# Half-row token products, a new order of the products, block 0's values turned on TensorE, and three MLP products moved forward, in a recurrent-memory transformer kernel

## The chip, the cores and the metric

One core of one Trainium2 chip. The time is the device time of one execution in microseconds (us). Medians of 3 to 6 timed executions are given, and one profiled execution of each kernel shows where the time lies (the one execution that was traced, so a stage of it can be unlucky). A ratio is the mean time of one kernel's fast runs over that of the other's in the same rounds, so it isn't quite the ratio of the medians quoted beside it.

## The reference, cut to what matters

```python
def _A_ref(x, mem0, Wq, Wk, Wv, Wo, seg_len):      # seg_len 32, 64 segments
    mem = mem0                                      # 8 memory rows
    for s in range(n_seg):
        h = concatenate([mem, x[:, s*32:(s+1)*32]])  # 40 rows of 512
        q, k, v = h @ Wq, h @ Wk, h @ Wv            # 32 heads of 128
        p = softmax(where(mask, q @ k.T * scale, -1e9))
        o = (p @ v) @ Wo
        mem = o[:, :8]                              # carried to the next segment
        outs.append(o[:, 8:])
h  = x + _A_ref(layernorm(x), ...)
h2 = h + gelu(layernorm(h) @ w1 + b1) @ w2 + b2     # MLP with 1792 inner columns
```

The segments form a chain through `mem`. The 64 segments come in 16 blocks of four (one block is 128 tokens). I call the four segments of a block its first to fourth.

## The kernel before

The kernel records every operation with its reads and writes, and a list scheduler places them on the five engines. TensorE's own order is fixed by hand in `ORDER`: Q0, K0, Q1, K1 are the projections (two halves of the heads), SC0 and SC1 the scores with the memory rows, SA the self scores of the tokens, V0 and V1 the value projections, PV0 and PV1 the value products of the memory rows, PVA the value product of the tokens (of the segment before), WO the output projection, and F a filler: projections for the next block, or WO of the last rows.

```python
PHASE = (109, 215, 114, 200)     # place of a segment's start within 256 instructions
ORDER = (("Q0", 0, 4), ("K0", 0, 4), ("Q1", 0, 4), ("K1", 0, 4), ("SC0", 0, 99), ("V0", 0, 4), ("V1", 0, 2), ("SC1", 0, 99), ("SA", 0, 99), ("V1", 2, 4), ("F",
         0, 2), ("PV0", 0, 99), ("F", 2, 3), ("PV1", 0, 99), ("WO", 0, 8), ("PVA", 0, 99), ("F", 3, 4))
# [...]
        def pv_a(s):                         # token value product: 8 pairs on the full array
            par = s % 3
            def f(e):
                for k in range(8):
                    ins = e.matmul(rows_a(k), VS[:, par, k // 4, (k % 4) * E:(k % 4 + 1) * E], BD[:, s % 2, k // 2, :, :, k % 2],
                                   start=(s == NS - 1 and k % 2 == 0), stop=True, skip_group_check=True)
                return ins
            S.op("pe", f, reads=[...], writes=QK, dur=0.45, mode=MF, ni=16)
# [...]
        def pv_a_ev(s):                      # one eviction of 768 columns
            ...
            S.either(copy2(ot, src, 768), reads=QK, writes=[("OTx", opar)])
# [...]
    def align(self):    # counts TensorE's instructions; pads the first passes of a segment with
        ...             # repeated weight loads until the count is PHASE[segment % 4] modulo 256
# [...]
        S.op("pool", lambda e: e.memset(maskR[:], 0.0), writes=["maskR"])   # then 18 affine selects
# [...]
            S.op("pool", lambda e: e.tensor_scalar(rs, ag[:, 1:2], 1e-5, None, ALU.add), ...)  # layer norm
```

`BONUS` adds a tuned number to the scheduler's priority for each kind of tile.

## Time and profile before

| | before |
|---|---|
| median of the runs | 850.03 us (849.67 to 851.71, 3 runs; 850.87 with a fourth) |
| span of the profiled run | 851.0 us, mean granted clock 0.990 |
| segment 4 starts at | 89.36 us |
| period of segments 4 to 59, mean / shortest | 10.88 / 10.68 us |
| segment 63 and the MLP tail | 118.67 us |

The prediction shows the lines behind this. They are read as start, duration, engine, source line, output<-input, partitions x columns, count. The bracket at the end is the engine's idle time before the row and what ended it; "issue" there means that the engine waited for nothing that the profile knows. Because matmuls overlap (in the trace of before a WO group starts at 303.31 and lasts 1.93 us, to 305.24, and the token product after it starts at 305.18), the distance between two starts (the advance) counts, not the duration.

### The profile page before, as it was taken

To read this page: it belongs to the slowest core of one execution; us is meant where nothing else is said; L and a number is where in the kernel's file an instruction comes from. 1 tells how busy PE (TensorE), PEld (TensorE's weight loads), DVE (VectorE), ACT (ScalarE), POOL (GpSimd) and SP (SyncE) were. 2 spreads that over 40 slices of the span, in tenths; PEclk is the share of its full clock that TensorE was granted. 3 is DMA by queue.
4 is the path that set the end of the run, shared out by engine and by line. 5 is a ranking of instruction groups with operands and counts; after the bars stand their busy time and mean duration, and the time that the engine had idled before them with its cause. 6 is when DMAs were issued, how large, how long until landed. Compare 5 with 4: busy or idle time off the path is not lost.

```text
span 851.0 us, 47411 instructions
## 1 busy us (share of the span) xinstructions
PE 801.9 (94%) x20061; PEld 438.9 (52%) x22307; DVE 566.5 (67%) x1818; ACT 553.2 (65%) x1561; POOL 265.3 (31%) x686
## 2 busy tenths in 40 slices
PE   3668999999999999999999999999999998999998
PEld 1245555555555555555555555555555555544443
DVE  3257677878787878777778777777777776633111
ACT  2446777767776767777777777777777776742442
POOL 5023114242424242424242333323232313166200
PEclk9979999999999999999999999999999999999999
DMA  9961000110101010101010101010112121274100
GB/s 344 361 193 22 10 17 22 30 29 23 35 20 38 17 40 16 35 22 35 23 35 22 35 23 35 17 29 17 28 35 54 47 72 35 70 195 111 50 25 25
DMA packets 66615, 48.80 MB, mean 57 GB/s; under 512 B 29156, under 2 KB 62828, under 8 KB 66412
## 3 DMA queue, kind: packets, MB, share of 16 engines
q1 hardware_dynamic: 66080, 45.50, 18.4%
q8 instruction: 166, 2.72, 1.3%
q10 hardware_dynamic: 332, 0.27, 0.1%
q14 instruction: 37, 0.30, 0.1%
HBM read 31.34 MB, written 8.39 MB: 47 GB/s over the span
## 4 chain that ended last, share of the span: by engine, by line
PE 84%; DMA 5%; DVE 3%; POOL 3%; SPq 2%; issue 2%; ACT 1%; ACTq 0%; POOLq 0%; DVEq 0%
PE ps L744 36%; PE ps L1009 13%; PE ps L490 10%; PE quad L1357 6%; PE ps L1350 4%; PE ps L1036 4%; PE quad L919 3%; PE quad L977 3%; DMA oN<-opT 2%; PE quad L889 2%; PE ps L947 2%; PE ps L1164 2%; POOL opT L1050 2%; SPq L671 1%; DMA xr<-in_A_x_dram 1%
## 5 line engine op out<-in xcount | busy, mean ns | idle before, releaser
L762 ACT CAST OT<-quad 128x128 bf16<-128x128 f32 (+1 forms) x192 | 85.2, 444 | 144.8 <-PE quad L977 86.5
L970 POOL COPY BD<-PTA 32x192 bf16<-32x192 bf16 x256 | 88.8, 347 | 245.7 <-DVE PTA L966 222.7
L1009 PE MATMUL ps<-WO,OT 128*32 128x256 bf16 x4224 | 130.5, 275 | 4.5 <-DMA WO<-in_A_Wo_dram 3.7
L744 PE MATMUL ps<-WV,hT 128*32 128x512 bf16 x1780 | 132.7, 381 | 0.0
L744 PE MATMUL ps<-WQ,hT 128*32 128x512 bf16 x1796 | 123.3, 385 | 5.8 <-DVE hT L1015 4.4
L762 ACT CAST kq<-ps 128x512 bf16<-128x512 f32 x160 | 92.5, 588 | 34.0 <-PE ps L744 32.1
L1009 PEld LDWEIGHTS ps<-WO,OT 128*32 128x32 bf16 x4224 | 107.1, 97 | 12.9 <-DMA WO<-in_A_Wo_dram 3.7
L744 PE MATMUL ps<-WK,hT 128*32 128x512 bf16 x1544 | 108.8, 385 | 0.0
L763 ACT ACTIVATE kq<-ps 128x512 bf16<-128x512 f32 x160 | 92.6, 600 | 21.1 <-PE ps L744 20.8
L742 PEld LDWEIGHTS <-hT 128*32 128x32 bf16 x3942 | 65.8, 98 | 59.3 <-DVE hT L1015 30.8
L785 DVE STREAM_TRANSPOSE KALL<-kq 128x256 f32<-128x256 f32 x160 | 69.0, 438 | 24.1 <-ACT kq L762 14.6
L901 ACT ACTIVATE EC<-quad,nmc 128x64 f32<-128x64 f32 x252 | 77.2, 313 | 2.5 <-DVE nmc L897 0.2
L762 ACT CAST VS<-ps 128x512 bf16<-128x512 f32 x127 | 74.4, 586 | 0.0
L960 DVE TENSOR_REDUCE sma<-SA 128x8 f32<-128x256 f32 x64 | 26.9, 420 | 71.1 <-ACT SA L959 71.1
L744 PEld LDWEIGHTS ps<-WK,hT 128*32 128x32 bf16 x1544 | 45.9, 97 | 43.3 <-issue 24.6
L785 DVE STREAM_TRANSPOSE QT<-kq 128x256 f32<-128x256 f32 x128 | 55.7, 435 | 18.7 <-ACT kq L763 17.4
L806 POOL COPY ZC<-QTB 128x256 bf16<-128x256 bf16 x64 | 25.3, 396 | 122.8 <-PE quad L889 63.3
L1353 ACT ACTIVATE WQ<-ps,b1t 128x512 bf16<-128x512 f32 x42 | 28.9, 688 | 51.9 <-PE ps L1350 51.9
L919 PEld LDWEIGHTS quad<-PTC,VS 32*128 32x128 bf16 x2048 | 24.1, 91 | 74.0 <-ACT EC L901 24.3
L744 PEld LDWEIGHTS ps<-WV,hT 128*32 128x32 bf16 x1780 | 41.7, 95 | 33.4 <-issue 21.0
L744 PEld LDWEIGHTS ps<-WQ,hT 128*32 128x32 bf16 x1796 | 48.1, 95 | 19.8 <-issue 8.8
L490 PE MATMUL ps<-WK,hT 128*32 128x512 bf16 x504 | 51.0, 382 | 0.0
(150 smaller groups left out, 1489.8 us busy)
## 6 DMA issues: line engine op xcount, KB each, us to landing
WV<-in_A_Wv_dram SPq DMA_DIRECT2D x4, 1024.0 KB, 10.4
WK<-in_A_Wk_dram SPq DMA_DIRECT2D x4, 1024.0 KB, 18.8
v_last<-VSB SPq DMA_DIRECT2D x64, 64.0 KB, 2.6
WQ<-in_A_Wq_dram SPq DMA_DIRECT2D x4, 1024.0 KB, 11.8
WO<-in_A_Wo_dram SPq DMA_DIRECT2D x16, 256.0 KB, 7.3
VBD<-v_last SPq DMA_DIRECT2D x64, 64.0 KB, 2.5
h_mid<-xr SPq DMA_DIRECT2D x16, 128.0 KB, 1.8
WQ<-h_mid SPq DMA_DIRECT2D x4, 512.0 KB, 4.4
```

Of the source, the lines that this page charges most:

```text
L490: return e.add_instruction(mybir.InstMatmult(name="I-%d" % (4000000 + _kept[0]), engine=mybir.EngineType.PE, start_tensor_calc=start, stop ...
L742: e.ldweights(l, tile_position=(0, 32 * j))
L744: ins = e.matmul(o, l, m, start=(k == 0), stop=(k == DC - 1), tile_position=(0, 32 * j), skip_group_check=True)
L762: return {"act": (lambda e: e.copy(out, src), t_act(n, ps_)), "dve": (lambda e: e.tensor_copy(out, src), 0.16 + 1.042e-3 * n * fast)}
L763: return {"act": (lambda e: e.mul(out, src, scale_), t_act(n, ps_)), "dve": (lambda e: e.tensor_scalar(out, src, scale_, None, ALU.mult), ...
L785: S.op("dve", lambda e: e.transpose(out, src), reads=[("kq", i)], writes=[key], dur=t_dve(256) + 0.02)
L901: ins = e.activation(EC[:, r, sl, :], o[:, sl, :], ACTF.Exp, bias=nmc[:, r, sl:sl + 1], accum_out=smc[:, r, sl:sl + 1])
L919: e.matmul(quad[:, j, (4 * r + i) * 16:(4 * r + i) * 16 + 16], VS[rows, s % 3, r, i * E:(i + 1) * E], PTC[rows, r, c0:c0 + 16, i // 2], st ...
L970: S.narrow(S.op("pool", lambda e, j=j, rows=rows: e.tensor_copy(BD[rows, par, :, j, :, :], PTA[rows, :, 0:NA, :]), reads=["PTA"], writes=[ ...
L1009: ins = e.matmul(ps[bank][32 * j:32 * j + 32, 0:256], lhs(slot(h)), wo_cols(h, b), start=(k == 0), stop=(k == 15), tile_position=(0, 32 * ...
L1036: ins = e.matmul(ps[bank][32 * j:32 * j + 32, :], OTB[:, bk % 2, slot(8 * j + q), :], WO[:, 8 * j + q, :], start=(q == 0), stop=(q == 7), ...
L1357: S.op("pe", lambda e: e.matmul(quad[:, t, :], gT_of(k, fc)[:, t * P:(t + 1) * P], W2[:, fc, :], start=(fc == 0), stop=(fc == FC - 1)), re ...
```

## The change

It is meant to take waits and work from TensorE in every segment (half-row token product, new order), to take block 0's round trip through DRAM out of the opening, and to do three MLP products in segments 60 to 62, where there is no filler, with the Gelus applied later to a 16-bit copy.

```diff
-PHASE = (109, 215, 114, 200)
+PHASE = (109, 219, 110, 219)
-BONUS = {"BD": -40, ... "maskA": -3.27, ... "maskR": 2.74, ...}
+BONUS = {... "BD": 6.72, ... "maskA": -20.65, ... "maskR": -40, ...}        # every entry re-tuned
-ORDER = (... ("SC0", 0, 99), ("V0", 0, 4), ("V1", 0, 2), ("SC1", 0, 99), ("SA", 0, 99), ("V1", 2, 4), ("F", 0, 2), ("PV0", 0, 99), ("F", 2, 3), ("PV1", 0, 99), ("WO", 0, 8), ("PVA", 0, 99), ("F", 3, 4))
+ORDER = (... ("SC0", 0, 99), ("V0", 0, 3), ("F0", 0, 1), ("V0", 3, 4), ("SC1", 0, 99), ("SA", 0, 99),
+         ("V1", 0, 4), ("F0", 1, 2), ("PV0", 0, 99), ("F0", 2, 4), ("PV1", 0, 99), ("WO", 0, 8), ("PVA", 0, 99), ("F1", 0, 4))
 START = (... "V", "X",
+         "S",                                       # v_B_turn: block 0's last-row values turned by 16 matmuls
 ...
-         ("B", "Q", 1, (1, 6)), ("T", "WO", 3, 8))
+         ("T", "WO", 3, 5), ("B", "Q", 1, (1, 6)), ("T", "WO", 5, 6), ("W", 7, 4), ("T", "WO", 6, 7), ("W", 7, 4), ("T", "WO", 7, 8))   # W: warm-up products
@@ lat
-            return HOP["sp"]
+            return HOP["sp"] if p.kind != "oN" else 4.4     # transposed read of the outputs
@@ pv_a
-                    ins = e.matmul(rows_a(k), VS[:, par, ...], BD[:, s % 2, k // 2, :, :, k % 2], ...)
+                    for t in range(2):
+                        rows = slice(64 * t, 64 * t + 64)
+                        o = quad[:, 2 * t + k // 4, 128 + 48 * (k % 4):176 + 48 * (k % 4)]
+                        ins = e.matmul(o, VS[rows, par, ...], BD[rows, s % 2, k // 2, 2 * t:2 * t + 2, :, k % 2],
+                                       start=(k % 4 == 0), stop=True, tile_position=(64 * t, 0), ...)
@@ pv_a_ev
-            S.either(copy2(ot, src, 768), reads=QK, writes=[("OTx", opar)])
+            for r in range(2):
+                S.either(copy2(ot, src, 384), reads=QK, writes=[("OTx", s % 2, r)])
@@ segments 60 to 62
+                    w1_first(sg, BANK["F1"], True)          # keep: 16-bit copy, Gelu later
@@ tail
-        for fc in range(FC):
+        for n, fc in enumerate(range(3, FC)):
             w1_first(fc, early[fc % 2])
+            if n < 3:
+                gelu_kept(n)
[cut: banks, the turn itself, keys of OTx, clears]
```

## The prediction

> **What bounds the kernel now.** I read the page first (busy table, slices), then TensorE's timeline over one segment, then the same microseconds on the other engines, then the opening and the end.
>
> ```profile
> PE 801.9 (94%) x20061; PEld 438.9 (52%) x22307; DVE 566.5 (67%) x1818; ACT 553.2 (65%) x1561; POOL 265.3 (31%) x686
> ...
> PEclk9979999999999999999999999999999999999999
> DMA  9961000110101010101010101010112121274100
> ```
>
> TensorE is the bound, DMA only in the first 50 us. "94%" hides waits, because ends are modelled, so I take start-to-start distances ("advance") from TensorE's timeline. One segment:
>
> ```profile
> 321.55 0.30 PE L889 MATMUL quad<-KALL,ZC 128*32 128x64 bf16 x16
> ...
> 322.98 0.31 PE L889 MATMUL quad<-KALL,ZC 128*32 128x64 bf16 x16
> ...
> 324.79 0.26 PE L919 MATMUL quad<-PTC,VS 32*128 32x16 bf16 x16
> 324.90 0.20 PE L923 MATMUL quad<-PTC,VBD 32*128 32x64 bf16 x4
> ```
>
> ```profile
> 303.31 1.93 PE L1009 MATMUL ps<-WO,OT 128*32 128x256 bf16 x64
> 305.18 0.52 PE L977 MATMUL quad<-BD,VS 128*128 128x96 bf16 x8
> 305.63 0.62 PE L1036 MATMUL ps<-WO,OTB 128*32 128x512 bf16 x8
> 306.26 1.06 PE L744 MATMUL ps<-WQ,hT 128*32 128x512 bf16 x16
> ```
>
> The period, start of Q0 to the next, is 10.68 us in about half of segments 4 to 59 and 10.88 in the mean. A 16-matmul pass advances 0.865. Eight filler matmuls ("F": next block's projections, or the last rows' WO product) should take 0.43 but advance 0.63 (305.63 to 306.26): 0.19 us of waiting for the memory rows, whose chain is
>
> ```profile
> 327.80 0.45 DVE L1021 STREAM_TRANSPOSE TT<-ps 128x256 f32<-128x256 f32 x1 [0.17 <-PE ps L1009]
> 328.28 0.39 DVE L1015 TENSOR_TENSOR hT<-TT 64x32 bf16<-64x32 f32 x2
> ```
>
> so Q0 cannot start before 1.08 to 1.09 us after the token value product starts (327.68 to 328.76). Three more bounds, measured from the first score product SC0 (321.55 = 0):
> - SC1: K's second half must be evicted and transposed.
> ```profile
> 322.39 0.45 DVE L785 STREAM_TRANSPOSE KALL<-kq 128x256 f32<-128x256 f32 x1
> ```
> That ends at 1.29; SC1 starts at 1.43. Where the transpose is late (segment 29: 1.68) SC1 follows 0.14 later (1.82). So SC1 is already exactly on that bound.
> - PV0 shares banks with SC1, so it follows the second exponential's end: in segments 61 and 62, which have no filler, TensorE sits idle and starts PV0 at 2.97 to 2.99. Elsewhere it arrives at 3.24.
> - PV1 follows PV0 by at least 0.79, the eviction of PV0's memory columns between them.
>
> The opening is paced by DMA, and its end runs at half clock:
>
> ```profile
> 20.60 7.06 DMA v_last<-VSB
> ...
> 45.41 6.78 DMA WO<-in_A_Wo_dram
> ```
>
> ```profile
> 35.00:40.00 5.00, 3.06 (x60) 1.15 (x52) 1.33 (x3) 2.62 (x6) 0.00 (x0) 1.00 1.13 270
> 40.00:45.00 5.00, 2.64 (x132) 1.41 (x128) 3.11 (x11) 3.85 (x16) 1.13 (x3) 1.00 1.11 322
> 45.00:50.00 5.00, 2.90 (x76) 1.46 (x64) 2.55 (x7) 1.48 (x4) 1.36 (x4) 0.93 1.10 348
> 50.00:55.00 5.00, 2.21 (x29) 1.07 (x54) 1.90 (x6) 0.00 (x0) 0.03 (x1) 0.50 0.67 207
> ```
>
> Last columns: clock, DMA share, GB/s. The queue carries 414 GB/s at 25 to 30 us, falls to 270 while block 0's last rows come back, and then 348 while WO arrives.
>
> [...]F before PV0 advances 0.98 instead of 0.87, some 0.1 per switch. [...] Here sixteen 32-row products advance 0.11 us (324.79 to 324.90): 27 ns per set of four. [...] Here 1.28:
>
> ```profile
> 743.27 1.28 ACT L1168 ACT_TABLE_LOAD   x1
> ```
>
> **The change part by part.**
>
> 1. Token value product: eight full-array pairs become sixteen 64-row pairs, two concurrent. Now it advances 0.45: 8 x 45 ns = 0.36 and 0.09 of switch. After: eight sets of two at about 25 ns[...], 0.20, with the switch about 0.30. Saves 0.15 of TensorE's work per segment. Its one eviction (0.80 us) becomes two, some 0.2 us more for ScalarE at 65%; nothing waits for it within a segment.
>
> 2. New order. Between SC0 and SC1 stand 20 matmuls (1.08 us) and SC0's 0.12 instead of 24: TensorE arrives at 1.20, but the K bound stays 1.43, so a new 0.23 us wait. Then 0.12 + 0.26 (self scores) + 0.865 (V1) + 0.215 (F) + 0.11 (switch) put PV0 at 3.00, beside its bound of 2.98; PV1 at 3.80 to 3.84; WO 0.24 later, 4.06; the token product 1.86 later, 5.92; then 0.30 and a whole filler pass 0.865, at 7.09 the next Q0 (the hT bound, 5.92 + 1.09 = 7.01, is covered). Before it was 7.22. Gain 0.13 us, not the 0.15 + 0.19 that removing both would suggest: the hT wait is paid back as a K wait. Times 56 segments: -7.3. Segments 1 to 3 have no filler: nothing.
>
> 3. Transposed output read (oN): the old scheduler assumed 2.0 us, the page's DMA list says 3.8. VectorE stood in its add up to SC1 in segments 29, 33, 37, 41, 45, 49, 57 (SC1 late by 0.36+0.36+0.48+0.07+0.68+0.49+0.26 = 2.7 us). With 4.4 the add moves behind the K transpose: -2.7. Other irregular stalls, up to 1.1 us inside one product without a semaphore (instruction supply, I think), come to a similar sum; new phases may move them: -1.0, a guess.
>
> 4. Opening: 0.52 MB of round trip leaves the queue: 0.26/0.41 + 0.26/0.348 = 1.4 us, and the dip (78 x 5 + 26 x 5 = 520 KB at 348) 1.5 us; with the shorter line for WO I take -3.5. The transpose on TensorE (16 matmuls of 256 columns, about 1.8 us) fits into its idle 5 us. Warm-up matmuls between the last WO quarters should keep the clock: segment 1 needs 6.1 us from Q0 to SC0 against 3.46, 2.65 us; at 8 chances in 10, with little else, -2.5.
>
> 5. Three MLP products move into segments 60 to 62, after the token product, where TensorE waits 1.08 anyway: 0.30 + 0.865 + 0.1 (switch) = 1.27, +0.18 each, +0.5; in the tail 3 x 0.865 goes: -2.6. But the built kernel's ScalarE list puts two of the deferred Gelus between the exponentials of segments 62 and 63: five late table loads, not one. Four more are 5.1 us of ScalarE. One comes before SC0's exponential in segment 63 and delays it about 1.5 us, one before PV1's eviction holds WO's second half about 1.0; about 0.3 from late Q and K evictions: +2.8. So part 5 is +0.7.
>
> 6. Segment 60 took 12.49, with a stall and a half-clock stretch; fewer idle gaps may avoid it: -0.9 (half of 1.8).
>
> Sum: -7.3 - 2.7 - 1.0 - 3.5 - 2.5 + 0.7 - 0.9 = -17.2, so 832.8. The sizes came from measured searches, as the tuned constants suggest; I lean slightly below: **831.5 us**.
>
> **Rivals.**
> - Every wait taken really goes: 0.34 x 56 = 19 us in the segments, about 820 in all. For it: the order looks tuned. Against it: SC1's 0.14 distance in stalled and smooth segments alike.
> - The balanced bounds collide (PV0, PV1 and Q0 each within 0.1 of another engine), ScalarE's extra eviction pushes, and the segment stays at 10.68: about 840. For it: ScalarE and VectorE at two thirds busy; against: their gaps around 326 to 328.
> - Clock stays half, or TensorE's opening waits for weights at the same times: 4 to 6 us of the opening stay, about 837.
> - Row tiles run one after another: the product then costs more than 0.45, and the gain per segment is gone. The 27 ns per set of four speaks against.
>
> **Range and chances.** Opening +-2.5, segments 56 x 0.06 = +-3.5, stalls +-3, tail +-2, together about +-6 at one deviation with what I have not seen: 822 to 841 for 8 in 10. The line for 2% is 833.0, just above my figure: faster 0.55, same 0.44, slower 0.01.
>
> **What would show it.** The token product advancing near 0.30; SC1 still 1.43 after SC0; no wait at the next Q0; most segments at 10.55; the last WO quarter near 49 us with clock 1.0 after it; SC1 no longer late every fourth segment; five table loads near 715 to 740, with a long segment 63. A period of 10.3, or SC1 at 1.2, would make me wrong on the low side; 10.68 on the high side.

No term of its sum is cut: -7.3 - 2.7 - 1.0 - 3.5 - 2.5 + 0.7 - 0.9 = -17.2, so 832.8. What the parts go on using is in the trace of before. "Switch" is the extra time at a change of tile shape: the full filler pass before PV0 advances 0.985 us instead of 0.865 (323.803 to 324.788). The 45 ns of part 1 are the distance of two full-array products there (most often 43 or 44 ns, in segments 4 to 59), the 25 ns that of two sets of four of the 32-row products (25 ns most often; 27 is the mean from 324.79 to 324.90). That pairs of 64-row products would keep this distance, and that warm-ups would keep the clock, were estimates; measured afterwards, from 50 to 55 us: 1.00 with warm-ups, 0.50 before.

## The result

The changed kernel took 847.27 us (846.32 to 847.68, 4 runs) against 850.87 of the kernel before on the same chip: ratio 0.9956, 95% interval 0.9938 to 0.9975. That is within 2%, and 6 us above the upper end of the predicted range of 822 to 841. A second occasion gave 845.44 against 852.60, ratio 0.9913 (0.9888 to 0.9937). So the change is worth 4 to 7 us, not 18.

The page of the changed kernel:

```profile
PE 795.7 (94%) x20597; PEld 427.3 (51%) x21748; DVE 578.3 (68%) x1826; ACT 575.6 (68%) x1626; POOL 267.1 (32%) x688
...
q8 instruction: 167, 2.74, 1.3%
```

TensorE's busy time fell by 6 us, as did the span (851.0 to 845.3). The mean clock is 0.996 instead of 0.990. TensorE's timeline, one segment of the changed kernel (segment 27):

```profile
340.44 0.30 PE L906 MATMUL quad<-KALL,ZC 128*32 128x64 bf16 x16
...
341.87 0.31 PE L906 MATMUL quad<-KALL,ZC 128*32 128x64 bf16 x16
...
346.36 0.37 PE L999 MATMUL quad<-BD,VS 64*128 64x48 bf16 x16
346.66 1.05 PE L1055 MATMUL ps<-WO,OTB 128*32 128x512 bf16 x16
347.54 0.82 PE L744 MATMUL ps<-WQ,hT 128*32 128x512 bf16 x12
```

Measured from SC0 (340.44): SC1 at 1.43, PV0 at 3.02 and PV1 at 3.81 (rows left out, at 343.46 and 344.25), the token product at 5.92 and advancing 0.30, the next Q0 at 7.10. Each is within 0.02 us of the prediction's part 2, and 21 of the 56 segments have this period of 10.55 us (to 0.015 us), the commonest though not "most", as the prediction had it. The steady segment is right. But another segment of the same trace has this inside PV1:

```profile
332.28 0.23 PE L938 MATMUL quad<-PTC,VS 32*128 32x16 bf16 x9
333.76 0.21 PE L938 MATMUL quad<-PTC,VS 32*128 32x16 bf16 x7 [1.25 <-issue]
```

The 16 small products of one operation are split by 1.25 us in which TensorE waits for no semaphore. The opening differs too. In the kernel before GpSimd builds the masks at once, and TensorE's timeline has its first V product at 14.39:

```profile
10.14 0.30 PE L850 MATMUL ps<-maskR,maskL 128*32 128x128 bf16 x4 [10.14 <-POOL maskL L611]
...
14.39 3.61 PE L744 MATMUL ps<-WV,hB 128*32 128x512 bf16 x32 [0.45 <-ACT hB L762]
```

GpSimd's timeline of the changed kernel: most of maskR stands behind the layer norm of token block 1 (`rst<-agg`), which has waited 3.62 us for VectorE's statistics, that is for the load of that block:

```profile
9.68 2.31 POOL L685 TENSOR_SCALAR rst<-agg 128x1 f32<-128x1 f32 x1 [3.62 <-DVE agg L684]
...
14.55 2.88 POOL L632 TENSOR_SCALAR_AFFINE_SELECT maskR<-maskR 128x8 bf16<-128x8 bf16 x9
```

TensorE's timeline of the changed kernel: its first product waits for maskR until 19.09 (before, until 10.14, for maskL, the last of its masks to be ready), and the first V product starts at 21.11, 6.7 us later than before:

```profile
19.09 0.30 PE L867 MATMUL ps<-maskR,maskL 128*32 128x128 bf16 x4 [19.09 <-POOL maskR L632]
...
21.11 3.61 PE L744 MATMUL ps<-WV,hB 128*32 128x512 bf16 x32 [0.45 <-ACT hB L762]
```

The end of the opening in stretches of 5 us (the last columns are clock, DMA share and GB/s):

```profile
40.00:45.00 5.00, 2.32 (x68) 0.88 (x56) 2.94 (x11) 4.04 (x16) 1.14 (x3) 1.00 1.09 348
45.00:50.00 5.00, 4.45 (x136) 3.30 (x136) 2.67 (x8) 1.38 (x5) 0.34 (x1) 0.66 0.95 295
50.00:55.00 5.00, 3.98 (x60) 1.71 (x101) 3.19 (x10) 0.61 (x2) 2.01 (x6) 1.00 0.33 90
```

The weights arrive earlier: 90 GB/s in the last stretch instead of 207, and the last piece of WO lands at 49.25 instead of 52.19 us. But its products (the last unit of WO) start at 52.44, as late as before (52.32), after a group of four warm-up products (L713):

```profile
51.48 1.04 PE L713 MATMUL ps<-WV,ident 128*128 128x512 bf16 x4
52.44 0.40 PE L1028 MATMUL ps<-WO,OT 128*32 128x256 bf16 x8
```

Segment 1, which follows, has the gain that the prediction expected from the clock: the granted clock from 55 to 60 us is 1.00 instead of 0.55, and from Q0 to SC0 it takes 3.52 us instead of 6.16. But it loses as much again. TensorE stalls inside a V product, and then WO runs while the clock falls to 0.50 (64 to 66 us): it advances 3.49 us, against 1.87 in another trace of the same kernel (e9).

```profile
61.04 0.86 PE L744 MATMUL ps<-WV,hT 128*32 128x512 bf16 x12 [1.39 <-issue]
...
63.08 3.55 PE L1028 MATMUL ps<-WO,OT 128*32 128x256 bf16 x64
```

The account of the two profiled runs, each line from the starts of the segments:

| | predicted | traces |
|---|---|---|
| regular period of segments 4 to 59, 56 x (10.546 - 10.679) | -7.3 | -7.4 |
| late add of the outputs | -2.7 | -2.7 |
| other stalls in segments 4 to 59 (the rest of 609.3 to 606.5) | -1.0 | +7.3 |
| opening and segments 1 to 3 (segment 4 at 89.36, then 88.70) | -6.0 | -0.7 |
| segments 60 to 62 | -0.4 | -1.2 |
| segment 63 and the tail (118.67, then 117.73) | +0.2 | -0.9 |
| sum | -17.2 | -5.6 |

Two lines make the miss: the stalls, off by 8.3, and the opening, off by 5.3.

The -0.7 of the opening is made of larger pieces: segment 1 starts 0.3 earlier (54.16, then 53.86), its part up to SC0 is 2.6 shorter, the rest of segment 1 is 3.1 longer (7.17, then 10.25: the stall and the half clock above), and segments 2 and 3 are 0.8 shorter. One trace of each kernel is thin here: in ten traces with the changed opening (the changed kernel, e2, e3, e6, e7, e9, e10, e11, e14, e16; table below) segment 4 starts at 85.61 to 88.70, 87.15 in the mean, and with the opening of before at 89.36 and 86.72 (e4). Segment 63 and the tail likewise: 118.67 before, but 117.86 in e4, which has nearly the same tail, so most of that -0.9 may be chance.

**What the stalls are.** In both traces, every stall without a semaphore in segments 4 to 59 stands at the same place modulo 256 in TensorE's stream of instructions: matmuls, weight loads and the semaphore instructions between them (number 193, counted from 0). The stall of 1.4 us in segment 1 above stands there too. The trace also has TensorE's instruction traffic: 167 packets of 16 KB on a queue of their own (q8), one for each 256 of its 42725 recorded instructions (before: 166 for 42698). I take these packets for the fetches of the instruction blocks. From them and the starts I computed, for blocks of the changed kernel:

```
segment  crossing into   next fetch starts  fetch    next crossing   gap between two
         a block at us   (us after it)      lasts    (us after it)   starts there
24       306.88          0.79               1.27     3.93            0.12
28       351.08          2.32               0.93     4.49            0.67
26       328.55          2.29               1.61     5.20            1.41
44       524.10          2.88               0.93     5.31            1.49
```

After a crossing the next fetch normally starts within 0.4 to 1.7 us (median 0.9). In some blocks it starts after 2.0 to 2.9 us. TensorE then goes on 1.2 to 1.5 us after that fetch has ended, and the gap that this leaves is the stall (0.12 in segment 24 is next to none). In the changed kernel's trace 15 of 140 fetches were late (over 1.8 us) and 15 crossings stalled over 0.3 us, each the next one after a late fetch; in the trace of before, 7 of 141 and 7. The stalls at crossings (the distance between two starts there, as far as it exceeds 0.13 us) sum to 5.6 us before and 10.7 us after, +5.1. The other +2.2 of that line is smaller: a crossing inside PV1 costs 0.06 to 0.15 us even when its fetch is in time, so the shortest periods of the four segments of a block are 10.69, 10.55, 10.61 and 10.55 (before: 10.74, 10.68, 10.68, 10.68), which makes 14 x (0.21 - 0.06) = 2.1. In e16 below, where the crossings drift, the four shortest are 10.59, 10.55, 10.55 and 10.55.

### The profile page after: what moved, and what is told of

Read it like the earlier page. It is cut to its first block, busy times and chain, and to the rows that moved or that the text cites. A ratio compares the mean times of both kernels' runs of the same rounds, so it can differ in the third digit from the quotient of the medians.

```text
span 845.3 us, 47501 instructions
## 1 busy us (share of the span) xinstructions
PE 795.7 (94%) x20597; PEld 427.3 (51%) x21748; DVE 578.3 (68%) x1826; ACT 575.6 (68%) x1626; POOL 267.1 (32%) x688
## 4 chain that ended last, share of the span: by engine, by line
PE 91%; ACT 3%; issue 2%; DVE 2%; POOL 1%; DMA 1%; ACTq 0%; POOLq 0%; DVEq 0%
PE ps L744 45%; PE ps L1028 15%; PE quad L1390 6%; PE ps L490 5%; PE ps L1383 4%; PE ps L1055 4%; PE quad L938 3%; PE quad L906 3%; PE quad L999 2%; PE ps L966 2%; PE ps L1188 1%; DMA xr<-in_A_x_dram 1%; PE quad L942 1%; ACT VS L762 1%; ACT kq L762 1%
## 5 line engine op out<-in xcount | busy, mean ns | idle before, releaser
L762 ACT CAST OT<-quad 128x384 bf16<-128x384 f32 (+1 forms) x255 | 95.1, 373 | 113.6 <-PE quad L999 74.9
L744 PE MATMUL ps<-WV,hT 128*32 128x512 bf16 x2032 | 144.4, 381 | 1.4 <-issue 1.4
L744 PE MATMUL ps<-WQ,hT 128*32 128x512 bf16 x1796 | 119.4, 379 | 3.3 <-DVE hT L1034 3.1
L763 ACT ACTIVATE kq<-ps 128x512 bf16<-128x512 f32 x160 | 95.1, 595 | 19.1 <-PE ps L744 14.8
L744 PE MATMUL ps<-WK,hT 128*32 128x512 bf16 x1544 | 105.5, 379 | 0.0
L744 PEld LDWEIGHTS ps<-WK,hT 128*32 128x32 bf16 x1544 | 41.7, 97 | 54.9 <-issue 28.5
L744 PEld LDWEIGHTS ps<-WV,hT 128*32 128x32 bf16 x2032 | 47.9, 96 | 19.8 <-issue 1.8
L938 PE MATMUL quad<-PTC,VS 32*128 32x16 bf16 x2048 | 37.2, 168 | 16.5 <-issue 9.4
L906 PEld LDWEIGHTS quad<-KALL,ZC 128*32 128x32 bf16 x2016 | 30.7, 96 | 41.5 <-ACT ZC L799 28.2
L914 DVE TENSOR_REDUCE nmc<-quad 128x2 f32<-128x128 f32 x126 | 34.5, 274 | 24.5 <-PE quad L906 24.5
## 6 DMA issues: line engine op xcount, KB each, us to landing
WQ<-in_A_Wq_dram SPq DMA_DIRECT2D x4, 1024.0 KB, 19.5
```

The source lines that it names most:

```text
L744: ins = e.matmul(o, l, m, start=(k == 0), stop=(k == DC - 1), tile_position=(0, 32 * j), skip_group_check=True)
L762: return {"act": (lambda e: e.copy(out, src), t_act(n, ps_)), "dve": (lambda e: e.tensor_copy(out, src), 0.16 + 1.042e-3 * n * fast)}
L763: return {"act": (lambda e: e.mul(out, src, scale_), t_act(n, ps_)), "dve": (lambda e: e.tensor_scalar(out, src, scale_, None, ALU.mult), ...
L906: ins = e.matmul(o[32 * j:32 * j + 32, sl, :], ZC[:, par, h, :], rhs, start=False, stop=(i == 3), tile_position=(0, 32 * j), skip_group_ch ...
L914: S.op("dve", lambda e: e.tensor_reduce(nmc[:, r, :], o, AX.X, ALU.max, negate=True), reads=[bkey], writes=[("nmc", r)], dur=0.28)
L938: e.matmul(quad[:, j, (4 * r + i) * 16:(4 * r + i) * 16 + 16], VS[rows, s % 3, r, i * E:(i + 1) * E], PTC[rows, r, c0:c0 + 16, i // 2], st ...
```

## The experiments

Runs of one kernel spread by 1.4 to 9.4 us, I think mostly through these stalls (not shown: one run of each was traced), so a stage is judged from its trace, and the whole time only where it moves by more. The stages spread too, as the column of segment 4 shows. This table is what the sixteen runs and the two kernels left; "late" counts fetches that start over 1.8 us after the crossing, in segments 4 to 59, and "stalls" is the sum at crossings there.

| run | median us | ratio to before (95%) | mean period | shortest | late | stalls us | segment 4 starts | 63 and tail |
|---|---|---|---|---|---|---|---|---|
| before | 850.0 | | 10.88 | 10.68 | 7 | 5.6 | 89.36 | 118.67 |
| after | 847.3 | 0.9956 (0.9938-0.9975) | 10.83 | 10.55 | 15 | 10.7 | 88.70 | 117.73 |
| e9 after again | 845.4 | 0.9913 (0.9888-0.9937) | 10.88 | 10.55 | 15 | 12.5 | 88.18 | 117.74 |
| e4 token alone | 850.3 | 0.9984 (0.9954-1.0013) | 10.89 | 10.65 | 6 | 5.1 | 86.72 | 117.86 |
| e7 order alone | 849.9 | 0.9978 (0.9955-1.0002) | 10.87 | 10.70 | 8 | 5.8 | 87.10 | 118.38 |
| e1 masks first | 850.1 | 0.9984 (0.9951-1.0018) | 10.86 | 10.55 | 13 | 11.9 | 85.94 | 117.73 |
| e12 no turn | 846.9 | 0.9924 (0.9894-0.9954) | 10.86 | 10.55 | 15 | 12.6 | 90.42 | 118.37 |
| e3 Gelu last | 850.4 | 0.9978 (0.9950-1.0005) | 10.96 | 10.55 | 20 | 16.7 | 87.66 | 116.27 |
| e11 add early | 846.8 | 0.9926 (0.9904-0.9948) | 10.84 | 10.55 | 15 | 11.1 | 85.61 | 117.74 |
| e2 phases of before | 851.8 | 0.9995 (0.9961-1.0029) | 10.95 | 10.55 | 18 | 17.9 | 86.05 | 117.94 |
| e6 phase 150 | 851.7 | 0.9987 (0.9963-1.0010) | 10.91 | 10.55 | 2 | 12.7 | 88.62 | 117.74 |
| e10 phase 116 | 846.4 | 0.9938 (0.9910-0.9966) | 10.82 | 10.55 | 13 | 10.2 | 87.33 | 117.74 |
| e14 phase 128 | 854.5 | 1.0025 (0.9999-1.0050) | 10.96 | 10.55 | 16 | 16.6 | 86.16 | 118.64 |
| e16 no pads | 858.1 | 1.0060 (1.0036-1.0085) | 11.05 | 10.55 | 17 | 21.1 | 86.11 | 117.73 |
| e8 first candidate | 846.6 | 0.9933 (0.9913-0.9953) | 10.90 | 10.56 | 5 | 12.5 | 85.03 | 117.09 |
| e13 second candidate | 841.9 | 0.9881 (0.9860-0.9902) | 10.81 | 10.55 | 11 | 9.6 | 84.33 | 115.64 |
| e15 third candidate | 848.3 | 0.9956 (0.9932-0.9981) | 10.88 | 10.55 | 17 | 13.0 | 85.27 | 115.63 |
| e17 fourth candidate | 852.2 | 0.9994 (0.9969-1.0019) | 11.01 | 10.55 | 13 | 19.5 | 85.46 | 116.87 |

All gave correct results. My theory after the first traces: the steady gain is real, and it is given back by stalls at the borders of instruction blocks and by an opening that waits for GpSimd's masks. Rivals: the stalls belong to the new order itself or to DMA traffic; the opening is still bound by WO.

### Token product and order, each alone

e4 puts the half-row product (with its layout and its eviction in halves) into the kernel before; e7 takes it out of the changed kernel.

```diff
 # e4, on the kernel before; e7 is the reverse on the changed kernel
+HALVES = (... "OTm", "OTx", "KB" ...)
+sc_place, pv_c, pv_a, pv_a_ev, keys of OTx as in the change; ORDER, BANK, PHASE, BONUS, START as before
```

> The kernel before with the half-row token value product alone (with its output's layout and its eviction in two parts); order, banks, phases and opening are those of the kernel before. Theory (step 2 of the prediction: the next segment's Q waits for the memory rows, 1.08 us after the token product starts, so without the new order the 0.15 us turns into waiting): the token product advances 0.30, the following filler advances about 0.78 instead of 0.63, the most frequent period of a segment stays at 10.66 to 10.70 us, and the time is 849 to 853 us, apart from instruction-block stalls that move. Rival (the product alone brings the gain): periods near 10.53 and a time of 842 to 845 us.

> The changed kernel with the old token value product put back (full-array products, one eviction), all else as in the changed kernel: the new order, banks, opening and MLP products. Theory (step 2 of the prediction: the order alone only moves 0.19 us of waiting from the next Q to the second score product): the token product advances 0.45, the second score product still starts about 1.43 us after the first, the next Q follows the filler without a wait, and the most frequent period is 10.68 to 10.71 us, 0.13 to 0.15 more than the changed kernel's 10.55. Rival (the order alone brings the gain): periods near 10.55.

TensorE's timeline of e4:

```profile
324.32 0.37 PE L982 MATMUL quad<-BD,VS 64*128 64x48 bf16 x16
324.62 0.40 PE L744 MATMUL ps<-WQ,hB 128*32 128x512 bf16 x4
324.85 0.39 PE L490 MATMUL ps<-WQ,hB 128*32 128x512 bf16 x4
325.41 1.06 PE L744 MATMUL ps<-WQ,hT 128*32 128x512 bf16 x16 [0.17 <-DVE hT L1017]
```

The product advances 0.30, and eight fillers then take 0.79 (324.62 to 325.41): Q waits for the memory rows, 1.09 us after the token product's start, as the prediction has it. The shortest period is 10.65, and 15 of the 56 are 10.67 to 10.70. TensorE's timeline of e7:

```profile
324.13 0.52 PE L994 MATMUL quad<-BD,VS 128*128 128x96 bf16 x8
324.58 1.05 PE L744 MATMUL ps<-WQ,hB 128*32 128x512 bf16 x16
325.46 1.04 PE L744 MATMUL ps<-WQ,hT 128*32 128x512 bf16 x16
```

SC1 is again 1.43 after SC0 (318.21 and 319.64 in the same segment), the product advances 0.45, there is no wait at Q, and the period is 10.70. So each part alone gains nothing and both together gain 0.13 us a segment. The expected periods held in both, and the expected time in e4 (849 to 853). The two also have 6 and 8 late fetches, like the kernel before with 7. The doubling to 13 to 20 came in every run that has both parts and the changed kernel's own phases.

### The changed kernel again

e9 is unedited, to see whether the same segments stall.

> The changed kernel itself once more, unedited, as the control of this call. If the stalls inside products are waits for instruction blocks whose fetch starts late by chance, they sit at the same places modulo 256 of TensorE's instruction stream as in the first trace (second value product of the first and third segment of each block of four, WO of the second), but in other segments than the first trace's 8, 22, 26, 28, 32, 37, 38, 40, 44, 48, 50, 52 and 56, and their sum differs by a few us from 10.7; runs spread by 2 to 6 us. If they are tied to what a given segment does (its stores, its loads), the same segments stall again. Time 846 to 853.

The time, 845.4, is just under the expected 846 to 853. In the first trace the first segments of blocks stalled in PV1 in segments 8, 28, 32, 40, 44, 48, 52 and 56, in this one in 8, 12, 32, 40 and 48; the third segments in 22, 26, 38, 50, now in 6, 18, 26, 38, 50, 58. The products and the place modulo 256 are the same (number 192: a record is missing), the segments are partly others. So a late fetch is partly chance, at fixed places. It isn't chance alone: among the first segments of blocks, in the six traces with this order, product and phases, segment 8 stalled in all six, 4 and 16 in none.

### Where the crossings lie

Five runs move the crossings, with nothing else changed on ScalarE, VectorE and GpSimd.

```diff
-PHASE = (109, 219, 110, 219)
+PHASE = (109, 215, 114, 200)   # e2    (150, 4, 150, 4)  # e6    (116, 219, 116, 219)  # e10
+PHASE = (128, 235, 116, 219)   # e14   ()  # e16: no padding loads
```

> The changed kernel with the four padding phases of the kernel before (109, 215, 114, 200 instead of 109, 219, 110, 219), which shift where TensorE's instruction stream crosses from one block of 256 instructions into the next. Theory (the stalls of 0.6 to 1.5 us inside the second token-and-memory value product in segments 4 to 59 are waits for the next instruction block): the stalls of the third segment of each block of four vanish or move to another product, always at the same place modulo 256 in the instruction stream; those of the first segment of each block stay as they are (same phase); the sum of such stalls goes from 10.7 us to some 6 to 8 and the time to 843 to 846. Rival (the stalls belong to the new order of the products, for instance a semaphore that the trace does not show): they stay in the same product of the same segments, and the time stays at 846 to 848.

In the second segments of blocks the stalls moved from WO to a semaphore wait before the token product; in the first and third segments they stayed in PV1, where the new crossing lies as well. All stand at number 192. They did not fall: 17.9 us, and the time, 851.8, missed the expected 843 to 846. The rival that the stalls belong to the order is refuted by this only in part; e6 and e16 below, with the same order and stalls in the K, V and Q products too, always at a crossing, refute it.

> The changed kernel with the padding phases 150, 4, 150, 4 in place of 109, 219, 110, 219: the same number of padding loads, but TensorE crosses into a new block of 256 instructions some 0.5 us before the first score product instead of inside it, and inside the second scores and self scores (where no fetch starts in any trace so far) instead of just after them. Theory (a fetch starts 0.5 to 1.2 us after a crossing unless the dense small products of the second scores and the self scores, 4.7 to 5.6 us after a segment's start, come in between, in which case it starts 2.2 us after and the next crossing stalls): late fetches become rare, the sum of stalls at crossings in segments 4 to 59 falls from 10.7 us to under 3, the mean period from 10.83 to 10.60 or 10.65, and the time is 8 to 12 us below the changed kernel's of this call. Rival (late fetches come from something else, DMA traffic or chance at any crossing): as many stalls at the new crossings, and the time within 3 us of the changed kernel's.

The half about late fetches held: 2 of 140 instead of 15. The half about the time failed. Crossings fell at 3.0 and 6.9 us after a segment's start, where the fetch starts only after 1.2 and 1.7 us (medians). With about 1.0 for the fetch and 1.3 until it is used, the latter makes 1.7 + 1.0 + 1.3 = 4.0, and the blocks there last 4.1 to 4.5 us with the stall: 32 smaller stalls, 12.7 us in all.

> The changed kernel with the phases 116, 219, 116, 219: TensorE crosses into the new block only some 5 to 9 instructions earlier, within the first score product, as the third segment of the kernel before does (there and in the run with the old token product, none of 42 fetches after that crossing was late, against 8 and 4 of 14 in the changed kernel). Nothing else differs, on no engine and not in the DMA queue. Theory (whether the fetch starts before the dense small products hangs on a few instructions): late fetches at that crossing become rare, the stalls in the second value product of the first and third segment of each block go from 7 to 11 us to under 3, the mean period from 10.83 or 10.88 to 10.65 to 10.72, and the time falls by 6 to 9 us against the changed kernel's 845 to 847. Rival (chance at any crossing in that stretch): stalls as before, time 845 to 850.

Expected was a fall of 6 to 9 us. In the third segments late fetches at that crossing fell to 1 of 14, in the first segments they stayed (9 of 14). The time, 846.4, is that of the changed kernel: the theory failed.

> The changed kernel with the phases 128, 235, 116, 219: the first segment of each block of four crosses into its new block some 12 instructions earlier again, at or before the start of the first score product; the third stays where the last run put it (1 late fetch of 14). Theory (position within a few instructions decides in the first segment too, and the last shift of 7 was too small there): late fetches after that crossing go from 7 or 8 of 14 to 2 or fewer, the stalls in the second value product of the first segment from 7 or 8 us to under 2, the mean period to 10.65 to 10.72 and the time to 838 to 842. Rival (in the first segment something else delays the fetch, not the place of the crossing): 5 to 9 of 14 still late, time 844 to 848.

In the first segments 3 of 14 were late instead of 8. But the third segments, whose crossing did not move against e10, went from 1 back to 7 of 14, and the second segments had 5 late fetches, with stalls in WO. The time, 854.5, is above both forecasts. So a few instructions do not decide it, and my rule falls; e10's good third segments were luck, or depend on the segment before.

> The changed kernel without any padding loads: some 625 TensorE instructions per segment instead of 640 in the mean, so the place of the crossing into a new block of 256 drifts through the segment, by some 30 instructions every two segments, and visits every place in turn. Theory A (late fetches belong to crossings in the stretch from the first to the second score products, 43, 32 and 29 of 100 at the three places in the traces so far, and near none elsewhere): few crossings fall there now, stalls come in runs of segments where a crossing lies 3 to 5.5 us after the segment's start, and their sum falls to 3 to 7 us; time 842 to 845. Theory B (any crossing can be late, the padded places are the good ones): stalls spread over the segment and sum to 12 us or more; time 848 or above.

This is the map. Without pads the crossing drifts through the segment. Sorted by its place (us after the segment's start), computed from the same records for 129 of the 135 crossings:

```
crossing at   crossings   late fetches   stalls that follow, us
0.0 to 3.0       16            0              0.1
3.0 to 3.5        7            1              1.8
3.5 to 4.0        7            7              6.1
4.0 to 5.0       12            0              4.2
5.0 to 6.0       23            6              4.3
6.0 to 7.0       11            1              4.1
7.0 to 11.5      53            2              0.5
```

Theory A's place is about right: 20.5 of 21.1 us follow crossings between 3 and 7 us after the start, from SC0 to PV1. In the changed kernel's trace 256 instructions that start there last 2.9 to 4.2 us, those that start in the second half of WO or after it 4.4 to 6.0. Its size is wrong. Crossings between 4 and 5 us stall by 4.2 us in all though none of their fetches is late. The time is the worst of all, 858.1; the pads are worth keeping.

### The opening

```diff
 # e1, on the changed kernel
-"maskA": -20.65, ... "maskR": -40
+"maskA": 30, ... "maskR": 40
 # e12 = e1 and, in START and v_B_out, block 0's values through DRAM as before
-"V", "X", "S", ("B", "V", 1, ...
+"V", "X", ("B", "V", 1, ...
-            if r == 1 and bk > 0:
+            if r == 1:
                 v_B_spread(bk)
+                chain[14:14] = spread["in", 0]
+                chain[8:8] = spread["out", 0]
```

> The changed kernel with one thing put back: GpSimd builds the two masks that TensorE's first products read (maskR, maskA) before its two layer-norm steps, as in the kernel before. The orders of TensorE, VectorE, ScalarE and the DMA queue are the same as in the changed kernel; only GpSimd's order differs. Theory (the opening became bound by TensorE, whose first product waits for maskR until 19.1 us): TensorE's first product near 10 us, its first V product near 14 to 15 instead of 21.1, the last WO unit near 47 to 49 us instead of 52.4, segment 4 starts at 83 to 86 instead of 88.7, and the whole kernel takes 841 to 844 us, 3 to 6 us less than the changed kernel's 847.3. Rival (the opening is still paced by the arrival of WO, and the late first product is hidden): the last WO unit stays within 1 us of 52.4 and the time stays at 846 to 848.

TensorE's timeline of e1:

```profile
12.90 2.75 PE L744 MATMUL ps<-WV,hB 128*32 128x512 bf16 x24 [0.45 <-ACT hB L762]
...
50.37 0.40 PE L1028 MATMUL ps<-WO,OT 128*32 128x256 bf16 x8
```

The first V product starts 8.2 us earlier, the last WO unit and segment 1 both 2.1 us earlier. The last WO unit, 50.37, misses the expected 47 to 49; segment 4 at 85.94 is inside the expected range, at its weak end. The theory of the masks holds up to segment 1, which starts at 51.79 here and at 52.65 to 54.68 in the ten traces with late masks: 0.9 to 2.9 us, not 3 to 6. At segment 4 it isn't shown, for four of those ten start it within 0.4 us of 85.94 (e11, e2, e14, e16). TensorE now waits for WQ at 35 us, and the clock falls to 0.50 from 40 to 45 us; and the last WO unit starts 1.6 us after its data landed (48.75), because a group of four warm-up products (results that nobody reads, to keep the clock up), 0.97 us together, stands before it. In e13, with half of them, it starts 0.1 us after its data (48.92, then 49.05). The whole time shows nothing of it (850.05, outside the expected 841 to 844 and above the rival's 846 to 848): the profiled run had 13 late fetches, and segment 60 took 13.49 us with a stall and a half clock.

> The changed kernel with the masks built first and block 0's last-row values sent through DRAM as in the kernel before, instead of turned on TensorE. It is to be compared with the masks-first run, whose last WO piece landed at 48.75 us and whose segment 4 started at 85.9. Theory (the round trip costs the DMA queue 2.9 us, 52.19 against 49.25 at the landing of the last WO piece in the traces of before and after): the last WO piece lands at 51.3 to 52.2, segment 4 starts 1 to 3 us later, at 87 to 89, and the time is 1 to 3 us above the masks-first run. Rival (the turn on TensorE costs what it saves): segment 4 starts within 0.7 us of 85.9.

The last piece of WO landed at 52.59 instead of 48.75, and segment 4 started at 90.42 instead of 85.94. That is 3.8 us for the queue and 4.5 for the opening once the masks don't hide it, more than I expected, in one trace of each. The queue's part is firm: the last piece lands at 48.53 to 49.57 in the fifteen traces with the turn and at 51.34 to 52.59 in the three without. The 4.5 is less so, given the spread of segment 4's start. The whole time doesn't confirm it: expected was 1 to 3 us above e1, and the ratio to the kernel before is below e1's (0.9924, 0.9984). They were run at other times.

### The Gelus

```diff
 # e3: gelu_kept and the tail's first Gelus
+            return [o for o in S.rec if o.kind in ("EC0", "EC1", "SA") and o.eng == "act"][-3:]
-                 ..., dur=0.65 + 1.3 * (fc == 0))
+                 ..., after=exps(), dur=0.65 + 1.3 * (fc == 0))
```

> The changed kernel with every Gelu of the first MLP block held until the last three exponentials are done, so that one late table load remains instead of five; the three MLP products themselves stay in segments 60 to 62. Theory (the four extra table loads cost about 2 us in segment 63 and the tail, as predicted for part 5): segment 63 shorter by 1.5 to 2.5 us, and the whole kernel takes 844.5 to 846 us. Rival (the loads are hidden, or the Gelus held back collect in the tail and delay TensorE there): within 0.7 us of the changed kernel's 847.3.

ScalarE's timeline of the changed kernel has five late table loads, at 725.22, 732.07, 735.86, 738.45 and 741.05. The second stands straight before the exponential of SC0 in segment 63; the third goes with a Gelu in front of PV1's eviction:

```profile
732.07 1.28 ACT L918 ACT_TABLE_LOAD   x1
733.36 0.31 ACT L918 ACTIVATE EC<-quad,nmc 128x64 f32<-128x64 f32 x1
```

In e3 one load is left, and segment 63 with the tail takes 116.27 instead of 117.73: -1.46, just below the expected 1.5 to 2.5. The other traces with this edit (the candidates) have 115.63 to 117.09, all below the 117.73 to 118.67 of those without: the effect is there, its size is 0.6 to 2.1. The whole time, 850.4, missed the expected 844.5 to 846; the trace has 20 late fetches.

### The late add

```diff
 # e11
-            return HOP["sp"] if p.kind != "oN" else 4.4
+            return HOP["sp"]
```

> The changed kernel with the scheduler's old assumption of 2.0 us for the transposed output read (instead of 4.4), which moves VectorE's late add of the outputs back ahead of the K transpose; TensorE's, ScalarE's and GpSimd's orders are the same. Theory (step 3 of the prediction): in some of the second segments of a block of four VectorE stands in that add and the second score product is late by 0.3 to 0.8 us there, 2 to 3 us in all; the time is 2 to 3 us above the changed kernel's. Rival (the read comes back in time in the new layout of windows): no such waits, and no difference beyond the spread of the instruction-block stalls.

VectorE's add stands ahead of the K transpose again, as before the change, and still SC1 is 1.43 to 1.44 after SC0 in all 56 segments; only two adds in the whole kernel wait for the read. The rival is right: the assumption of 4.4 is not what removed the 2.7 us. e4 and e7 point to the order: e4, with the order of before, still has eight late SC1 (3.9 us in all), e7, with the new one, none. Which part of the new order it is was not isolated.

### Candidates

```diff
 # e8: masks first, Gelus last, PHASE (150, 4, 150, 4), and
-("B", "Q", 0, (1, 4)), "Q1"
+("G", "Q", 0, (1, 4)), ("T", "G", 0, 2), ("W", 7, 8), ("T", "G", 2, 4), "Q1"     # warm-up at the wait for WQ
 # e13: e8 with PHASE (116, 219, 116, 219), and
-("T", "WO", 5, 6), ("W", 7, 4), ("T", "WO", 6, 7), ("W", 7, 4),
+("T", "WO", 5, 6), ("W", 7, 2), ("T", "WO", 6, 7), ("W", 7, 2),
 # e15: e13 with PHASE (128, 235, 116, 219);  e17: e13 without pads
```

> A candidate that should beat both kernels: the changed kernel with the masks built first, eight warm-up products while TensorE waits for the second half of WQ in the opening (so that its clock does not fall to half there), every Gelu held until the last exponential, and the phases 150, 4, 150, 4. If the theories are right: segment 4 starts at 83.5 to 86 us, the periods of segments 4 to 59 are 10.60 to 10.65 in the mean, segment 63 and the tail are 1.5 us shorter, and the time is 832 to 838 us, 13 to 18 us below the kernel before. If the stalls only move, 842 to 846.

> A second candidate: masks first, eight warm-up products at the wait for WQ, two instead of four warm-up products before each of the last two WO units (in the first candidate the last unit started 1 us after its data), Gelus held until the last exponential, phases 116, 219, 116, 219. If the theories hold: segment 4 starts at 83.5 to 85.5 us, the mean period of segments 4 to 59 is 10.65 to 10.72, segment 63 and the tail take 116.3 us, and the time is 836 to 840 us. If the phase does nothing: 843 to 846.

> The second candidate with the same phases 128, 235, 116, 219: masks first, warm-up at the wait for WQ, shorter warm-ups before the last WO units, Gelus last. If the first segment's fetches come in time, 833 to 838 us; if not, 840 to 843 as the second candidate (841.9).

> The second candidate (masks first, warm-up at the wait for WQ, shorter warm-ups at the end of the opening, Gelus last) without padding loads. Under theory A 836 to 840 us, under theory B 843 or above; the second candidate itself took 841.9.

e8 kept the clock at 1.00 to 40 us and 0.98 to 45 us and started segment 4 at 85.03; its stalls, 12.5 us, put it at 846.6, beyond even the 842 to 846 that it expected if the stalls only moved. e13 is the best: 841.93 us, ratio 0.9881 (0.9860 to 0.9902), with segment 4 at 84.33 and the tail at 115.64. It beats the kernel before, and the changed one by 3 to 6 us if the ratios to the kernel before (0.9956, 0.9913) are compared. They were run at other times. It misses its 836 to 840: 11 late fetches and 9.6 us of stalls are near the changed kernel's 15 and 10.7. Its shorter warm-ups may have a price: in e13 and e17 the clock falls after them (in e13 to 0.66 at 50 to 55 us) and segment 1 needs 5.21 us to SC0 instead of 3.52; in e15, with the same warm-ups, it doesn't (mean granted clock of the profiled run 0.998, against 0.996 in e13 and 0.997 in e17). e15 and e17 have the same changes in the opening and the tail and lose the gain with their phases: 13.0 and 19.5 us of stalls, 848.3 (expected 833 to 838, or 840 to 843) and 852.2.

## Why the prediction was wrong, point by point

- **Part 1 and 2, the segment: right.** The product advances 0.30, SC1 stays at 1.43, no wait is left at Q0, and the period is 10.55. The rival that every wait goes (10.3) and the rival that the segment stays at 10.68 are both out. e4 and e7 show that the two waits replace each other, as step 2 says. -7.4 us against -7.3. Sixteen 64-row products advance 0.30 us, against 0.45 for eight full ones, and their pairs start 25 ns apart (most often, in segments 4 to 59 of the changed kernel): the rival that row tiles run one after another, at more than 0.45, is out.
- **Part 3, first half: the size right by luck, the cause not.** The late SC1 disappeared, -2.7; e11 shows that 4.4 was not needed for it.
- **Part 3, second half: wrong, the step that failed most.** "Other irregular stalls ... (instruction supply, I think) ...; new phases may move them: -1.0, a guess." I read their sum in the kernel before as near 2.7; counted as above it is 5.6. The cause was named rightly, but I treated it as noise that a tuned kernel would have reduced. It grew by 7.3 us: +5.1 in late fetches (7 to 15) and +2.1 from crossings inside PV1. Late fetches doubled only where both parts are present (e4 has 6, e7 has 8), and why is not shown. That a faster segment leaves a block less time explains what a late fetch costs, not how often one comes: after the crossings 3.5 us into the first and third segments e7's blocks last as long as the changed kernel's (3.82 and 3.78 us, against 3.82 and 3.79), with 5 and 0 late fetches of 14 against 8 and 4. I also gave the stalls a deviation of 3 us; they came out 8.3 us from the forecast, nearly three times that.
- **Part 4, the opening: the DMA gain and the clock gain right, the path wrong.** The last WO piece landed 2.9 us earlier (predicted 3.5; 3.8 between e12 and e1), but segment 1 started only 0.3 earlier. I read the new order of TensorE and the queue and not that of GpSimd. Its new priorities put the masks behind a load, TensorE's first V product started 6.7 us later and TensorE became the bound of the opening, and the warm-ups before the last two WO units, 0.97 us a group, now stood on the path. The clock gain came as predicted, 2.6 us from Q0 to SC0 in segment 1 (predicted 2.5), and all ten traces with the changed opening have it (3.52). But the stall and the half clock later in segment 1, 3.1 us, took it back; that is the step of the irregular stalls again. Nor is all of the 2.6 the change's: with the opening of before, e4 needed 4.82 there and not 6.16. So -6.0 became -0.7, in the trace that has the latest segment 4 of its ten.
- **Part 5: pessimistic.** Segments 61 and 62 grew by 0.27 and 0.22 (predicted 0.18 each). The four extra loads cost 1.5 us by e3, not 2.8; segment 63 and the tail gained 0.9 instead of losing 0.2 (against e4's tail only 0.1).
- **Part 6, segment 60:** 12.49 became 10.75, -1.7 (predicted -0.9). This is luck: e4, with the order of before, has 10.74, and with the new order it took 13.49 in e1 and 11.70 in e9.
- **The lean** of 1.3 us towards "measured searches" was wrong as well: the searches that I guessed behind the tuned constants didn't show in the stalls, which differ from run to run.

What stays open: what makes a fetch start 2.0 to 2.9 us instead of 0.9 us after a crossing, and why that became twice as frequent. In the changed kernel's first trace no packet of the kernel's own transfers was under way between crossing and fetch in 14 of the 15 late cases (and in 95 of the 125 others), and neither the place within a few instructions (e10, e14) nor the number of the segment settles it.

## What to carry to other kernels

When an engine's stream is long and dense, look for waits at the borders of its blocks of instructions: count how long the shortest 256 instructions last (here 2.9 us) and compare it with the fetch's delay, length and time until use (here 0.9, or 2.0 to 2.9 when late, then 1.0 and 1.3 us). Don't book stalls of a kind that you can't explain as a gain: here they took back most of one. Compare the order on every engine, also one that is off the critical path: a tuned priority on GpSimd moved TensorE's first product by 9 us. And where one cause makes runs spread by several us, judge a part of a change by its stage in the trace.
